# Attention into a gated feed-forward kernel: batch 2's casts moved to steps 34 to 38 and shared by two engines, a check moved to step 17, and a first weight load of four column blocks

## The chip, the cores and the metric

The kernel runs on one core of a Trainium2 chip. The metric is the device time of one execution in microseconds (us). Runs of one kernel are compared by their median. A profiled execution leaves a trace; its span is the time from the first to the last recorded instruction.

The core's engines run their own instruction queues, each in order, and wait for each other through semaphores: TensorE (PE) multiplies, VectorE (DVE), ScalarE (ACT) and GpSimd (POOL) work elementwise, and SyncE (SP) issues transfers. ScalarE and GpSimd issue transfers too, in their own order among their other instructions.

## The reference

Eight batches of eight heads, 576 positions, 64 wide. Each head has causal attention with a decay taken from `s`; the heads' outputs side by side give 4608 rows of 512, which go through an RMS norm and a gated feed-forward layer of width 1536.

```python
scores = scale * np.matmul(q, k.transpose(0, 1, 3, 2))
cum = np.cumsum(np.maximum(s, 0.0), axis=-1)
bias = -(cum[:, :, :, None] - cum[:, :, None, :])
scores = np.where(causal, -1000000000.0, scores + np.minimum(bias, 0.0))
attn = softmax(scores)                       # exp of the scores less their maximum, over the sum
x = (attn @ v).transpose(0, 2, 1, 3).reshape(4608, 512)
...
xn = x / np.sqrt(np.mean(x * x, axis=-1, keepdims=True) + 1e-06) * rms_g
g = xn @ w_gate
out = (g * (1.0 / (1.0 + np.exp(-g))) * (xn @ w_val)) @ w_out
```

All inputs and the output are float32. The kernel multiplies in bfloat16.

## The kernel before, in words

**Chunks and steps.** The 4608 rows form nine chunks of 512, worked through by `ffn(c)` one after another. A chunk has 12 pairs of groups on TensorE, the gate group (L737) and the value group (L746), four products of 512 columns each, and then an output part of four row blocks with 12 products each (L759). A group fills one of four PSUM buffers `psF`. ScalarE makes `T` from the gate group (tanh, L740), VectorE makes `U` from `T` and the same buffer (L749) and `Ht` from `U` and the value group (L742, L754); the output part reads `Ht` block by block, and ScalarE takes its result out (L764). So a buffer of the ring of four comes free when `U` or `Ht` has read it.

Between the groups the attention of later batches is woven in. `ffn` calls `step()` 36 times in a chunk: after each group, and three times in each block of the output part. Steps are numbered through (`slot`); steps 1 to 36 belong to chunk 0, 37 to 72 to chunk 1. In steps 30 to 33 of chunk 0 the GpSimd list is left out.

**What a step does.** It writes, in this order: what the last score step left over; one scaling of a finished row block (`x_scale`, L386, VectorE) with its transpose by DMA on SP (`xt_dma`, L397); one entry of ScalarE's list `act_side`; one transpose of the next batch's queries or keys by DMA on SP (`kq_dma`, L179) where no scaling moved; an entry of the load list `v_side` in odd steps, of GpSimd's list `pool_side`, then TensorE's attention work (`place`), and an entry of VectorE's list `dve_side`. Each list is first in, first out; an entry goes when its condition holds, otherwise the list waits. All of this is fixed when the program is written: a step is a place in the engines' orders, and at run time an engine stands only for data.

**Attention work on TensorE.** `do_s` makes a score step (L275) in the single buffer `psS`, ScalarE takes the exponentials (L299), and GpSimd masks the diagonal block (`affine_select`, L308). `do_av` multiplies with the values (L341, L347), VectorE divides (L354, L356), the sum of squares is taken on ScalarE (L363) or, for the first blocks, on VectorE (L367), and GpSimd makes the row factor (`alpha`, L376 and L379), which `x_scale` needs. Rows go to `xnT` by a DMA transpose, but for block (1, 3) by TensorE (`do_xt`, L406, evicted by L415). `need(c)` sees to it that a chunk's last block is in `xnT` before the chunk starts.

**Batch 2's keys and queries.** They are loaded as float32 into `kq32` by GpSimd's queue (`load2`, L129 and L135; `w` is 1 for q, 0 for k) and cast to bfloat16 into `kqn` (`cast_x`, L153, five for q; `cast`, L145, five for k). `casts(2)` puts all ten on GpSimd's list: those of q from eight steps after their load, those of k behind them. `kqn` is shared by batches 0 and 2, so the casts must come after the check of batch 0. When q is done, `over(1)` frees five `kq_dma` of batch 2, at most one in two steps, and the load of batch 3's q from ScalarE's queue; `over(0)` does the same for the keys, which TensorE transposes (`do_t`, L192, L200) from step 41 on. A load entry that `early` has put up goes only in the first 23 steps of a chunk, and three steps after the load before it.

The steps of this kernel, followed through the conditions, are: casts of q in steps 25 to 29, of k in 34 to 38; `kq_dma` of batch 2 in 33, 35, 37, 42 and 44; score steps of batch 2 from step 46; loads of batch 3 in 37, 40, 43 and 46, its casts from 47 to 57.

**The check.** `check(b)` keeps the largest magnitude of what was cast: one `check_mag` (L418) and two `check_max` (L424) of VectorE, in odd steps. For batch 0's keys they come in steps 9, 11 and 13.

**The weights.** Before chunk 0, GpSimd's queue loads w_gate's column blocks 0 to 3 (exclusive) and later 3 to 6 (`load_w`, L771); the rest follows in step 1. Gate group fb of chunk 0 reads block fb.

Of the kernel before, what the change touches and what calls it, by code (L numbers as in the profile page):

```python
# [12 lines left out]
AF = mybir.ActivationFunctionType  # L13
# [13 lines left out]
def kernel(  # L27
# [12 lines left out]
    nc = tc.nc  # L40
    B, H, S, D = q.shape
# [20 lines left out]
    wg_sb = pers.tile([128, CC, DF], BF16, name="wg_sb")  # L62
# [84 lines left out]
    def cast_x(eng, b, w, hp):  # L147

        if hp < HP:
            o = kqn[:, b % 2, w, 0:4].rearrange("p r h d -> p (r h d)")[:, hp * 512:hp * 512 + 512]  # L150
            o = o.rearrange("p (r h d) -> p h r d", r=4, h=2)
            i = kq32[:, w, 2 * hp:2 * hp + 2, 0:256].rearrange("p h (r d) -> p h r d", d=D)
            eng.tensor_copy(out=o, in_=i)  # L153
        else:
            cast(eng, b, w, 4, 5)

# [24 lines left out]
    def load_v(b, c):  # L181
        n = rows(c)
        nc.gpsimd.dma_start(  # L183
            out=v_sb[0:n, b % 2, c, :, 0:64],
            in_=v[b, :, c * 128:c * 128 + n, :].rearrange("h p d -> p h d"))
# [241 lines left out]


    SLOTS = 36
    slot = [0]  # L430
    first, chunk = [0], [0]
    done = {}
# [10 lines left out]
    pool_side, dve_side, v_side, act_side = [], [], [], []  # L443
# [5 lines left out]
    def ready(lag, *key):  # L449
        return at(*key) + lag <= slot[0]  # L450
# [16 lines left out]
    def check(b, ws=(1, 0)):  # L467
        t = slot[0] + (8 if b >= KB else 0)

        def when(w):  # L470
            if b < 2:
                return slot[0] % 2 and chunk[0] == b and slot[0] > 8
            return phase() >= 25 and slot[0] >= t and (w == 0 or ready(0, "cast", b, 1))
        dve_side.extend((lambda w=w: when(w), f) for w in (ws if b < KB else (0, 1)) for f in (
            lambda w=w: check_mag(b, w), lambda: check_max(0), lambda: check_max(1),
            lambda w=w: done.__setitem__(("check", b, w), slot[0])))
# [18 lines left out]
    def casts(b):  # L495

        def key(c):
            load_k(b, c)  # L500
            done["K", b, c] = slot[0]
            if c == NSC - 1:
                check(b)

        def over(w):
            done["cast", b, w] = slot[0]
            if b + 1 < B and (w == 1 or b + 1 < KB):
                loads(b + 1, w, early, 4)
            if w == 1:
                x_seq.extend((b, ww, c) for c in range(NSC) for ww in ((1, 0) if b >= KB else (1,)))  # L510
            else:
                done["cast", b] = slot[0]
                check(b)

        def free(w):
            return ready(0, "check", b - 2, w) and (
                ready(0, "T", b - 2) if w == 0 and b < KB + 2 else
                b < XB + 2 or ready(4, "X", b - 2, w, 4))
        if b >= KB:
            pool_side.extend((lambda: free(0) and slot[0] % 2 == 0, lambda c=c: key(c)) for c in range(NSC))  # L520
        fns = [(1, lambda r=r: cast_x(nc.gpsimd, b, 1, r)) for r in range(NSC)]
        if b == 2:
            fns[-1] = (1, lambda: (cast_x(nc.gpsimd, b, 1, NSC - 1), over(1)))
        else:
            fns += [(1, lambda: over(1))]
        if b < KB:
            fns += [(0, lambda r=r: cast(nc.gpsimd, b, 0, r, r + 1)) for r in range(NSC)]
            fns += [(0, lambda: over(0))]
        pool_side.extend((lambda w=w: ready(8 if b == 2 else 7, "raw", b, w) and free(w), f) for w, f in fns)

    def after_tail(b):
        if b + 2 < B:
# [129 lines left out]
    def step(bare=False):  # L662
# [15 lines left out]
        run_side(act_side)  # L678

        if not moved and x_seq and slot[0] - last["X"] >= 2 and not (  # L680
                scaled[0] < len(x_list) and ready(1, "AV", *x_list[scaled[0]], 1)):
            b, w, c = x_seq[0]
            if (ready(2, "cast", b, 1) and ready(1, "S", b - 2, 4, 0)
                    and (w == 1 or ready(7, "K", b, c))):
                x_seq.pop(0)
                kq_dma(b, w, c)
                done["X", b, w, c] = last["X"] = slot[0]
                if b >= KB and (w, c) == (0, NSC - 1) and b + 2 < B:
                    casts(b + 2)
# [79 lines left out]
    def load_w(src, dst, f0, f1):  # L769
        fs = slice(f0 * 128, f1 * 128)  # L770
        nc.gpsimd.dma_start(out=dst[:, :, fs],  # L771
                            in_=src[:, fs].rearrange("(cc p) f -> p cc f", p=128))
# [79 lines left out]
    with tc.manual_schedule():  # L852
# [63 lines left out]
        load_v(0, 2)  # L916
        load_v(0, 3)
        load_v(0, 4)
        load_w(moe_w_gate, wg_sb, 0, 3)
        do_t((0, 0, 0), pT=psT(), dve=False)  # L920
        do_t((0, 1, 0), pT=psF16(), dve=False)
        stir(2)
# [57 lines left out]
        norms += [do_av((0, 3, 1), psT32(), act=True, apart=True)]  # L980
        norms[3](False)
        alpha(3, 4)
        load_w(moe_w_gate, wg_sb, 3, 6)
        warm(4)
        for qb in range(4):
            x_scale(0, qb, gq)
# [16 lines left out]
        def load2(w):  # L1003
            load_kq(nc.gpsimd, 2, w)
            load_kq_tail(nc.gpsimd, 2, w)
            done["raw", 2, w] = slot[0]

        def put(queue, n, *fns):
# [12 lines left out]
        put(v_side, 7, lambda: (load_v(1, 0), load_v(1, 1)))  # L1021
        put(v_side, 11, lambda: (load_wout(0), load_wout(6)))
        later(v_side, 0, [
            lambda: load_v(1, 2), lambda: load_v(1, 3), lambda: load2(1), lambda: load_v(1, 4),
            lambda: load2(0)])

        check(0, (0,))
# [194 lines left out]
```

## Time and profile before

| what | value |
|---|---|
| runs | 371.28, 367.72 and 371.75 us; median 371.28 |
| profiled execution | 367.71 us, span 366.1 us |
| TensorE products busy | 346.9 us, 95% of the span |
| VectorE, ScalarE, GpSimd busy | 275.2, 237.6, 179.5 us |
| chunk 0 on TensorE | from 26.47 to 69.98 us |
| TensorE's clock | 0.996 of full speed |

A line of the timeline has the start and the duration in us, the engine, the line of the kernel, the operation with what it writes and reads, how many of the same kind were merged, and in brackets the idle time of the engine before it with what ended it. A line of the waits says who waited for whom, the total in us, how often, and the longest. The busy time of TensorE counts a product up to its modelled end, while the next one has already started, so that gaps show better between starts.

### The profile page before, as it was taken

Reading aid. Unit: us, or ns where it says so; the run is one execution under the profiler, and the core shown is the slowest. Engines: PE = TensorE matmul, PEld = TensorE weight load, DVE = VectorE, ACT = ScalarE, POOL = GpSimd, SP = SyncE. Lnnn points to the kernel's source line nnn. Section 1 sums busy time; section 2 is a strip of 40 time slices with the busy share of each in tenths; the row PEclk is TensorE's granted clock in tenths of the full one; section 3 lists DMA queues with packets and bytes.
Section 4 is the critical chain, followed back from the end, with each engine's and each line's share of the span. In section 5 each row is a group of like instructions: output and inputs, shape, how many; then the busy total and the mean of one; then the engine's idle time right before and its main releaser. Section 6 shows DMA issues by size and latency. Waiting matters only on the chain. (4 is left out here: it accounts for less than half of the span.)

```text
span 366.1 us, 6930 instructions
## 1 busy us (share of the span) xinstructions
PE 346.9 (95%) x2337; PEld 161.4 (44%) x2383; DVE 275.2 (75%) x523; ACT 237.6 (65%) x614; POOL 179.5 (49%) x288
## 2 busy tenths in 40 slices
PE   5989999899999999999999999999999999999992
PEld 2444445443444444444444444444444444444441
DVE  6696997599887889789989789884588557827820
ACT  3978876367885788776787776777677644223311
POOL 7959766949556465879648923732222200000000
PEclk9999999999999999999999999999999999999998
DMA  7999999999969399949969944981300130020011
GB/s 232 134 234 245 172 207 216 176 217 208 195 138 107 67 191 142 166 114 167 164 196 166 152 103 109 114 90 55 105 14 17 43 109 1 0 88 29 1 60 60
DMA packets 124096, 45.81 MB, mean 125 GB/s; under 512 B 103956, under 2 KB 118808, under 8 KB 124056
## 3 DMA queue, kind: packets, MB, share of 16 engines
q0 software_dynamic: 62688, 14.29, 48.4%
q1 hardware_dynamic: 51872, 23.80, 32.2%
q10 hardware_dynamic: 9496, 7.23, 8.3%
q8 instruction: 19, 0.31, 0.4%
q14 instruction: 21, 0.17, 0.2%
HBM read 37.90 MB, written 9.44 MB: 129 GB/s over the span
## 5 line engine op out<-in xcount | busy, mean ns | idle before, releaser
L299 ACT ACTIVATE E<-psS,biasK 128x256 bf16<-128x256 f32 (+3 forms) x328 | 107.3, 415 | 19.7 <-PE psS L275 19.3
L737 PE MATMUL psF<-xnT,wg_sb 128*128 128x512 bf16 x418 | 109.9, 380 | 2.2 <-DMA wg_sb<-in_moe_w_gate_dram 0.5
L746 PE MATMUL psF<-xnT,wv_sb 128*128 128x512 bf16 x419 | 110.1, 379 | 1.2 <-DVE U L749 0.3
L759 PE MATMUL psF<-wout_sb,Ht 128*128 128x512 bf16 x416 | 99.7, 379 | 0.6
L749 DVE SCALAR_TENSOR_TENSOR U<-T,psF 128x512 bf16<-128x512 f32 x108 | 73.6, 682 | 30.6 <-ACT T L740 30.6
L740 ACT ACTIVATE T<-psF 128x512 f32<-128x512 f32 x108 | 64.5, 597 | 43.4 <-PE psF L737 40.9
L308 POOL TENSOR_SCALAR_AFFINE_SELECT E<-E 128x512 bf16<-128x512 bf16 x64 | 45.2, 706 | 83.2 <-ACT E L299 82.8
L742 DVE TENSOR_TENSOR Ht<-U,psF 128x512 bf16<-128x512 bf16 x99 | 67.7, 684 | 7.0 <-PE psF L737 0.5
L737 PEld LDWEIGHTS <-wg_sb 128*128 128x128 bf16 x432 | 38.7, 98 | 46.3 <-issue 6.5
L746 PEld LDWEIGHTS <-wv_sb 128*128 128x128 bf16 x432 | 38.6, 98 | 43.0 <-issue 5.0
L759 PEld LDWEIGHTS <-Ht 128*128 128x128 bf16 x432 | 38.7, 98 | 42.0 <-issue 2.3
L764 ACT ACTIVATE osb<-psF 128x512 f32<-128x512 f32 x36 | 21.4, 595 | 35.6 <-PE psF L759 29.5
L386 DVE SCALAR_TENSOR_TENSOR xs_sb<-x_sb,al_all,g_row 128x512 bf16<-128x512 bf16 (+1 forms) x36 | 29.9, 829 | 13.7 <-POOL al_all L379 12.6
L183 POOL DMA_DIRECT2D v_sb<-in_v_dram x40 | 35.8, 897 | 0.3 <-PE psAV L347 0.2
L363 ACT ACTIVATE xs_sb<-x_sb 128x512 bf16<-128x512 bf16 (+1 forms) x37 | 23.5, 636 | 16.8 <-DVE x_sb L356 16.4
L424 DVE TENSOR_TENSOR acc<-acc,mag 128x1280 bf16<-128x1280 bf16 x32 | 28.4, 899 | 0.2
L275 PE MATMUL psS<-kqT 64*128 64x256 bf16 (+2 forms) x304 | 25.9, 256 | 2.1 <-ACT E L299 0.8
L347 PEld LDWEIGHTS <-E 128*128 128x128 bf16 x320 | 21.7, 98 | 10.1 <-issue 0.2
L379 POOL TENSOR_TENSOR al_all<-al_all,mhalf 128x1 f32<-128x1 f32 (+2 forms) x39 | 22.4, 574 | 3.2
L341 PEld LDWEIGHTS <-E 128*128 128x128 bf16 x256 | 20.0, 98 | 7.7 <-DVE x_sb L356 0.6
L275 PEld LDWEIGHTS <-kqT 64*128 64x128 bf16 x320 | 9.3, 94 | 31.1 <-issue 30.1
L376 POOL TENSOR_SCALAR al_all<-ss_all 128x1 f32<-128x1 f32 (+2 forms) x39 | 10.1, 260 | 24.5 <-ACT xs_sb L363 19.7
(125 smaller groups left out, 301.1 us busy)
## 6 DMA issues: line engine op xcount, KB each, us to landing
out_dram<-osb SPq DMA_DIRECT2D x36, 256.0 KB, 2.3
kq<-in_q_dram ACTq DMA_DIRECT2D x5, 1024.0 KB, 8.4
v_sb<-in_v_dram POOLq DMA_DIRECT2D x32, 128.0 KB, 7.1
kq<-in_k_dram SPq DMA_DIRECT2D x4, 512.0 KB, 5.3
kq<-in_q_dram SPq DMA_DIRECT2D x4, 512.0 KB, 7.2
kqn<-in_k_dram POOLq DMA_DIRECT2D x16, 128.0 KB, 5.0
wout_sb<-in_moe_w_out_dram POOLq DMA_DIRECT2D x2, 768.0 KB, 10.0
kq<-in_q_dram POOLq DMA_DIRECT2D x1, 1024.0 KB, 13.6
```

What stands on the lines that cost most here:

```text
L183: nc.gpsimd.dma_start(out=v_sb[0:n, b % 2, c, :, 0:64], in_=v[b, :, c * 128:c * 128 + n, :].rearrange("h p d -> p h d"))
L275: nc.tensor.matmul(pair[par][:, j * W:j * W + M], lhsT=kT, rhs=qT, start=(j == 0 and not premask), stop=(j == nj - 1))
L299: nc.scalar.activation(out=eo, in_=ei, func=AF.Exp, scale=0.125, bias=biasK[:, kb, bh:bh + 1])
L308: nc.gpsimd.affine_select(out=Ev[:, :, 0:nq], in_=Ev[:, :, 0:nq], pattern=[[0, nh], [1, nq]], compare_op=ALU.is_ge, fill=0.0, base=0, chan ...
L386: nc.vector.scalar_tensor_tensor(out=xs_sb[0:n, (b * NSC + qb) % NX, :], in0=x_sb[0:n, (b * NSC + qb) % NX, :], scalar=al_all[0:n, col:col ...
L424: nc.vector.tensor_tensor(out=acc[:, sl], in0=acc[:, sl], in1=mag[:, sl], op=ALU.max)
L737: nc.tensor.matmul(Gp, lhsT=wg_sb[:, cc, fs], rhs=xnT[:, cc, x0:x0 + DM], start=(cc == 0), stop=(cc == CC - 1))
L740: nc.scalar.activation(out=T, in_=Gp, func=AF.Tanh, scale=0.5)
L742: nc.vector.tensor_tensor(out=Ht[:, fb - 1, :], in0=pend[0], in1=pend[1], op=ALU.mult)
L746: nc.tensor.matmul(Vp, lhsT=wv_sb[:, cc, fs], rhs=xnT[:, cc, x0:x0 + DM], start=(cc == 0), stop=(cc == CC - 1))
L749: nc.vector.scalar_tensor_tensor(out=U, in0=T, scalar=1.0, in1=Gp, op0=ALU.add, op1=ALU.mult)
L759: nc.tensor.matmul(Op, lhsT=Ht[:, fb, tb * 128:(tb + 1) * 128], rhs=wout_sb[:, fb, :], start=(fb == 0), stop=(fb == FB - 1))
```

## The change

The ten casts of batch 2 wait for step 34 (`K2`), one entry per step and engine. ScalarE takes q's head groups 3 and 4 and k's row sets 0, 1 and 2; GpSimd takes q's groups 0, 1 and 2 and k's row sets 3 and 4. The wait for the load's step is gone; the wait for the data stays. `over` is called with the last GpSimd entry of q and of k. The transposes of batch 2 may start one step after that instead of two, and are not held back for the row block (1, 4). The check of batches 0 and 1 starts after step 16 instead of 8 (for batch 1 this changes nothing, its chunk starts later). The first part of w_gate has four column blocks, the second two. On the load list the last value block of batch 1 goes ahead of batch 2's q, which is thereby issued in step 19 instead of 17.

```diff
             i = kq32[:, w, 2 * hp:2 * hp + 2, 0:256].rearrange("p h (r d) -> p h r d", d=D)
-            eng.tensor_copy(out=o, in_=i)
+            if eng is nc.scalar:
+                eng.activation(out=o, in_=i, func=AF.Copy)
+            else:
+                eng.tensor_copy(out=o, in_=i)
...
+    K2 = 34
...
             if b < 2:
-                return slot[0] % 2 and chunk[0] == b and slot[0] > 8
+                return slot[0] % 2 and chunk[0] == b and slot[0] > 16
...
-        pool_side.extend((lambda w=w: ready(8 if b == 2 else 7, "raw", b, w) and free(w), f) for w, f in fns)
+        if b == 2:
+
+            def put2(queue, *fs):
+                queue.extend((lambda: slot[0] >= K2 and free(0) and free(1), f) for f in fs)
+            put2(act_side, *[lambda r=r: cast_x(nc.scalar, b, 1, r) for r in (3, 4)],
+                 *[lambda r=r: cast(nc.scalar, b, 0, r, r + 1) for r in (0, 1, 2)])
+            put2(pool_side, *[lambda r=r: cast_x(nc.gpsimd, b, 1, r) for r in (0, 1)],
+                 lambda: (cast_x(nc.gpsimd, b, 1, 2), over(1)),
+                 lambda: cast(nc.gpsimd, b, 0, 3, 4), lambda: (cast(nc.gpsimd, b, 0, 4, 5), over(0)))
+            return
+        pool_side.extend((lambda w=w: ready(7, "raw", b, w) and free(w), f) for w, f in fns)
...
         if not moved and x_seq and slot[0] - last["X"] >= 2 and not (
-                scaled[0] < len(x_list) and ready(1, "AV", *x_list[scaled[0]], 1)):
+                scaled[0] < len(x_list) and x_list[scaled[0]] != (1, 4) and ready(1, "AV", *x_list[scaled[0]], 1)):
...
-            if (ready(2, "cast", b, 1) and ready(1, "S", b - 2, 4, 0)
+            if (ready(1 if b == 2 else 2, "cast", b, 1) and ready(1, "S", b - 2, 4, 0)
...
-        load_w(moe_w_gate, wg_sb, 0, 3)
+        load_w(moe_w_gate, wg_sb, 0, 4)
...
-        load_w(moe_w_gate, wg_sb, 3, 6)
+        load_w(moe_w_gate, wg_sb, 4, 6)
...
-            lambda: load_v(1, 2), lambda: load_v(1, 3), lambda: load2(1), lambda: load_v(1, 4),
+            lambda: load_v(1, 2), lambda: load_v(1, 3), lambda: load_v(1, 4), lambda: load2(1),
             lambda: load2(0)])
```

## The prediction

> **What bounds the kernel now.** I read four views: the page, TensorE's waits between 26 and 110 us, the timeline of 60 to 70 us, and the landing times of single transfers. Times "at 33.38" are those of the profiled execution before.
>
> ```profile
> span 366.1 us, 6930 instructions
> ...
> PE 346.9 (95%) x2337; PEld 161.4 (44%) x2383; DVE 275.2 (75%) x523; ACT 237.6 (65%) x614; POOL 179.5 (49%) x288
> ```
>
> TensorE sets the time; no other engine is above 75%. So an edit is worth only the TensorE gap that it closes. Where those gaps lie, the waits of 26 to 110 us say (in total, times, longest):
>
> ```profile
> PE psT L406 <- DVE xs_sb L386: 1.0, 1, 1.0
> PE psF L737 <- DMA wg_sb<-in_moe_w_gate_dram: 0.5, 1, 0.5
> PE psF L737 <- DVE U L749: 0.4, 1, 0.4
> PE psF L746 <- DVE U L749: 0.3, 1, 0.3
> PE psF L737 <- DMA xnT<-xs_sb: 0.3, 1, 0.3
> PE psF L737 <- ACT xnT L413: 0.3, 1, 0.3
> PE psT L217 <- DVE xnT L415: 0.2, 1, 0.2
> ```
>
> Six of the seven lie in chunk 0 or at its end, one in chunk 1. From 110 us on TensorE idles about 1 us up to the last chunk, so nothing big is to be had there. These rows understate the gaps, because a product is counted busy until its modelled end, 0.38 us after its start. I measure from start to start instead: four 512-column products take 0.87 (33.38 to 34.25), four transposes 0.22 (34.25 to 34.47), eight value products 0.25, four 0.13, and a score step 0.33 before the next group starts (49.76 to 50.09).
>
> The longest gap has a story, which the timeline of 60 to 70 us tells (start, duration, what; idle before it and what ended it):
>
> ```profile
> 60.55 0.61 POOL L153 CAST kqn<-kq 128x512 bf16<-128x512 f32 x1 [1.16 <-DMA kq<-in_q_dram]
> ...
> 61.57 0.19 ACT L363 ACTIVATION_READ_ACCUMULATOR xs_sb<-x_sb 128x1 f32 x1
> ...
> 61.69 1.72 POOL L153 CAST kqn<-kq 128x512 bf16<-128x512 f32 x3
> 63.50 0.19 POOL L376 TENSOR_SCALAR al_all<-ss_all 128x1 f32<-128x1 f32 x1
> 64.28 0.60 POOL L145 CAST kqn<-kq 128x512 bf16<-128x512 f32 x1
> 64.97 0.51 POOL L376 TENSOR_SCALAR al_all<-ss_all 128x1 f32<-128x1 f32 x1
> 66.15 1.12 DVE L386 SCALAR_TENSOR_TENSOR xs_sb<-x_sb,al_all,g_row 128x512 bf16<-128x512 bf16 x1 [0.72 <-POOL al_all L379]
> 67.33 0.40 PE L406 MATMUL psT<-ident_bf,xs_sb 128*128 128x128 bf16 x4 [1.02 <-DVE xs_sb L386]
> ```
>
> The sum of squares of block (1,2) is ready at 61.76, but GpSimd, in order, is in the casts of batch 2 until 63.4; its factor comes at 63.50. Block (1,3) queues behind that and one more cast. So its scaling starts at 66.15, stretched to 1.12 us beside the factors and casts (0.74 where GpSimd is idle), and TensorE's transposes wait.
>
> **Part 1, w_gate.** Column block 3 now comes with the second part, issued at 24.3 and 9.1 us on its way, so it lands at 33.4. Group 3 could start at 32.42 + 0.22 = 32.64 and starts at 33.38. With block 3 in the first part (issued 14.3, landed after 6.8) the **0.74 us** go. Bounds of the price: the queue behind carries a third more, between 0 and 6.8/3 = 2.3 us. w_val's first half (issued 16.1, 8.9 on its way: 25.0) is needed at 27.33, so even 2.3 is covered. The first keys of batch 1 (21.6 + 5.3 = 26.9) are cast at 28.02; at 2.3 they would hold ScalarE 1.2 and TensorE's transposes of 30.25 at most 0.5. I take 0, since the part lands 5 us before use, and keep 0.5.
>
> **Part 2, the check in step 17.** One mask and two maxima (0.81, 0.80, 1.25 = 2.86 us of VectorE) leave 36.9 to 45.3, where VectorE is busy 13.68 of 14 us and runs two groups behind. Three TensorE gaps come from that: 41.56 + 0.33 = 41.89 against 42.28 (0.39); 45.52 + 0.13 = 45.65 against 45.91 (0.26); 46.87 + 0.33 = 47.20 against 47.50 (0.30). Sum **0.95**. The work lands in steps 17 to 21 (46.9 to 54). Laying VectorE's instructions out anew there, without the old backlog and with three more of 0.81, the last Ht (56.49 to 57.18 now) ends at about 57.9. The output group needs it as its twelfth product, at 58.84, or 58.6 once the gap of 47.50 is gone: 0.7 us of cover, and 0 lost. Between 36 and 46 the sum of VectorE's work falls from 10.3 to about 7.5 of 10.5 us, so no new gap there.
>
> One row of the old place is a warning: a maximum took 1.25 us beside an affine select (43.80) and, at 83.99, 2.27 beside casts, but 0.80 beside weight loads being issued (40.83). The Trainium skill, "SBUF — State Buffer", section "Who interferes with whom", says that a VectorE instruction with two SBUF inputs contends with GpSimd instructions that read SBUF, not with those that only write. The trace agrees (2.27 against 0.80). By that rule both maxima can meet a select in steps 19 and 21; at 1.25 each the last Ht would be 0.9 later and cost TensorE 0.2.
>
> **Part 3, the casts.** Ten on GpSimd (about 0.61 each) become five there and five on ScalarE. One of 512 columns on ScalarE has no row: one of 256 takes 0.41 and twice that, 0.81, bounds it from above; the 512-column eviction of L764 at 0.60 has the same form, and I take 0.6, together 3.0 us. They fall in steps 34 to 38 (66 to 73), where ScalarE idles 3.45 us before L764 at 69.54, 0.92 before 71.06 and 1.29 before 72.94: free. Without that cover T of chunk 1 slips; the psF ring of four bears about 1.7 us.
>
> GpSimd is free from step 25 to 33. The factor of (1,2) can follow at 61.8 to 62.6, its scaling at 63.2 behind the evictions of (1,3), its transpose at 64.0 instead of 65.46. For (1,3): squares 63.97, factor 64.8, scaling 65.6. TensorE comes at 63.55 + 12 x 0.217 = 66.15: the gap of 67.33 - 66.15 = 1.18 goes. The first group of chunk 1 could start at 69.29 + 0.25 = 69.54 and waits until 69.98 for the transpose of (1,2) (0.44). Its transpose took 4.5 us; 64.0 + 4.5 = 68.5 against 69.54 - 1.18 = 68.36 leaves 0.14. Gain **1.48**.
>
> The loads: q of batch 2 is issued in step 19 instead of 17 (about 50.0 for 46.9). It took 13.6, so 63.6 at most, before step 34. k stays at 54.0 + 11.6 = 65.6, before step 36 (68.5 on this scale). Both are waited for by five ScalarE instructions now, with L764 and T queued behind.
>
> What is late next: batch 2's cast of q ends in step 36, not 29. Its five transposes on SP move from steps 33, 35, 37, 42, 44 to 37, 39, 42, 44, 46 (the (1, 4) exemption lets the second go at 39). SP runs ahead, so the first two start when the casts end, near 69; the third stays behind the transpose of (1,4), as now the fourth does (77.60). Scores of batch 2 keep their steps (46, 50, 53), since the keys' casts end in step 38, one earlier. The second transpose has about 7.7 us, the third 10.3 - 0.5. Landings here were 4.8, 6.3 and 10.3: a wait of 0 (6.3) to 2.6 (10.3 for both). I take **0.3**, near the first.
>
> The loads of batch 3 move three steps (q to 40 and 43, k to 46 and 49), its casts from 47-51 and 53-57 to 50-54 and 56-60. So the maximum of step 49 no longer meets them: it took 2.27 and held the group that could start at 85.51 + 0.87 = 86.38 until 86.91, **0.53**, bounds 0 and 0.53. The tail of batch 4's q misses its last step in chunk 1 (phase below 24) and goes from step 59 to 73; its casts wait behind the key loads anyway, 80 for 79. Later transposes shift by one or two steps, five or more ahead of their scores.
>
> **The sum.** 0.74 + 0.95 + 1.48 + 0.53 = 3.70, less 0.3: 3.4 us. The profiled execution took 367.71 (span 366.1 and 1.6 around it): **364.3**. Its runs are 367.72, 371.28 and 371.75, so the profile is the low one and the median 3.6 above. Part of that spread should be these very waits (GpSimd stood 1.16 us for a transfer at 60.55 with everything behind it), which no longer sit on the path. I carry half over: a median of **366.0**, between 364.3 and 367.9.
>
> **Rivals.** (1) Half of the gain is eaten by VectorE in steps 17 to 24: each instruction of the check at 1.25 and a late factor (L376 waits for VectorE's squares, then holds the selects) make the last Ht about 1.7 us late beyond its cover. 366.0 by the profile, some 367.5 as a median. For it: VectorE is nearly full from 51.3 to 59. Against: 0.7 of cover, and VectorE needs only 2.03 of 2.50 us after 57.5.
> (2) Slower: batch 2's transposes. SP starts them later, among the v loads, q and k of batch 3. TensorE, in order, stands at the score step of 79.74 or 87.87. Each us above 7.7 on the way costs one; from 11.4 us the gain is gone, and at 15 the profile is 367.71 + 3.6 = 371.3, the median 373. For it: one took 10.3 in that traffic. Against: the two issued before it took 4.8 and 6.3, and batch 3's q now starts later.
> (3) Nothing to tell: the gaps close, but ScalarE stands for k in steps 36 to 38. TensorE loses from a landing 4.5 us later than now, all of it from 8 us. Then 367.7, median about 371. Against: the longest landing of such a load is 13.8.
>
> **Numbers.** Forecast 0.62, rivals 0.18, 0.12 and 0.08. One per cent, 3.7 us, is about what a measurement of this kernel can tell from no change. Against 371.28 the line is 367.6: the forecast is below it in most cases (0.53 of 0.62), rival 1 in less than half (0.07): faster 0.6. Above 375.0 only rival 2 comes, and only with landings of some 19 us (0.06): slower 0.06, the rest, 0.34, within. Range 363.0 (all gains, a low median) to 370.0 (rival 1 and part of rival 2).
>
> **What would show it.** Right: L737 no longer waits for wg_sb; no wait of L406 near 66; L376 right behind L363; chunk 1 starting near 66.7 instead of 69.98; no maximum above 1.3 us. Wrong: a wait of L275 for kqT by DMA, of L759 for Ht near 57, or ScalarE waiting for kq.

## The result, and the profile after

| | before | after |
|---|---|---|
| median | 367.76 us (366.56 to 371.75) | 366.12 us (364.10 to 369.53) |
| ratio of the times, 95% interval | | 0.9951 [0.9927, 0.9975] |
| profiled execution | 367.71 us (span 366.1) | 364.69 us (span 363.0) |

The change makes the kernel half a per cent faster. The median of before is 367.76 us over all its runs; of the three shown ahead of the prediction, two lay high (371.28 and 371.75). The profiled execution of before stands at its median, that of after 1.4 us under its own. So the two traces differ by 3.0 us and the medians by 1.6, and what the traces show is compared stage by stage below.

The page after, and TensorE's waits between 26 and 110 us (total, times, longest):

```profile
span 363.0 us, 6976 instructions
...
PE 348.8 (96%) x2383; PEld 160.5 (44%) x2383; DVE 273.4 (75%) x523; ACT 239.8 (66%) x619; POOL 178.2 (49%) x283
```

```profile
PE psT L344 <- DVE x_sb L359: 0.4, 1, 0.4
PE psF L751 <- ACT xnT L416: 0.3, 1, 0.3
PE psF L751 <- DVE rZ L357: 0.2, 1, 0.2
PE psS L278 <- ACT E L302: 0.2, 1, 0.2
```

Lines have moved: L737 is now L751, L759 is L773, L406 is L409, L386 is L389, L376 is L379, L356 is L359. Of the seven rows of before, the waits for `xs_sb`, for `wg_sb`, for `U` (two rows) and for `xnT` by DMA or VectorE are gone by name. The wait for `xnT` by ScalarE stays; it ends as chunk 0 begins. New are the first row, TensorE waiting for VectorE's eviction of `x_sb`, and the third, which stands at the start of chunk 1 and is explained below.

The other engines' busy time has hardly changed (VectorE 275.2 to 273.4, ScalarE 237.6 to 239.8, GpSimd 179.5 to 178.2), so the gain should be idle time of TensorE. Its own busy sums can't be compared: the trace before has 2337 product records and that of after 2383. Where the gain lies, the time from each chunk's first gate product to that of the next says, taken from the timelines:

| chunk | 0 | 1 | 2 | 3 | 4 |
|---|---|---|---|---|---|
| before | 43.51 | 39.19 | 38.73 | 38.38 | 37.84 |
| after | 41.62 | 38.65 | 38.89 | 37.73 | 37.43 |
| difference | -1.89 | -0.54 | +0.16 | -0.65 | -0.41 |

In the trace after, chunk 0 starts 0.32 later (26.79 for 26.47), which arises before the weight load is issued; from chunk 5 on the two differ by no more than 0.1. With that start the sum is -3.0, the difference of the profiles.

The end of chunk 0, in the timeline after (PEld is TensorE's weight load for the product behind it):

```profile
57.88 0.76 PEld L773 LDWEIGHTS <-Ht 128*128 128x128 bf16 x5 [0.55 <-DVE Ht L768]
...
58.41 0.69 DVE L370 SCALAR_TENSOR_TENSOR xs_sb<-x_sb 128x512 bf16<-128x512 bf16 x1
...
59.20 0.19 POOL L379 TENSOR_SCALAR al_all<-ss_all 128x1 f32<-128x1 f32 x1 [2.28 <-DVE rZ L357]
...
60.01 0.62 POOL L311 TENSOR_SCALAR_AFFINE_SELECT E<-E 128x512 bf16<-128x512 bf16 x1
60.07 1.11 DVE L389 SCALAR_TENSOR_TENSOR xs_sb<-x_sb,al_all,g_row 128x512 bf16<-128x512 bf16 x1 [0.41 <-POOL al_all L382]
...
61.31 0.42 DVE L359 TENSOR_TENSOR x_sb<-psT,rZ 128x256 bf16<-128x256 f32 x1
...
61.79 0.20 PE L344 MATMUL psT<-v_sb,E 128*128 128x65 bf16 x1 [0.44 <-DVE x_sb L359]
...
63.73 0.50 POOL L379 TENSOR_SCALAR al_all<-ss_all 128x1 f32<-128x1 f32 x1 [0.34 <-ACT xs_sb L366]
...
64.90 0.75 DVE L389 SCALAR_TENSOR_TENSOR xs_sb<-x_sb,al_all,g_row 128x512 bf16<-128x512 bf16 x1 [0.71 <-ACT E L302]
...
65.83 0.39 PE L409 MATMUL psT<-ident_bf,xs_sb 128*128 128x128 bf16 x4
...
68.41 0.55 PEld L751 LDWEIGHTS <-wg_sb 128*128 128x128 bf16 x4 [0.35 <-DMA xnT<-xs_sb]
68.41 1.04 PE L751 MATMUL psF<-xnT,wg_sb 128*128 128x512 bf16 x4 [0.23 <-DVE rZ L357]
```

GpSimd now makes the factor of the last block, (1, 3), right behind ScalarE's sum of squares (63.73), its scaling ends at 65.65, and TensorE transposes it at 65.83 with no wait. The casts of batch 2 follow behind, from 66.12 on GpSimd and from 65.66 on ScalarE, 0.62 us each. But the chain ahead has a new gap at 61.79: VectorE's squares of block (1, 1) come late (58.41), GpSimd stands 2.28 us for their sum at 59.20 (the bracket names another VectorE row, L357), the scaling that follows takes 1.11 beside an affine select, and the eviction at 61.31 holds the products. The first row shows a smaller wait ahead of it, of the output part for the last `Ht`.

The first group of chunk 1 still starts late, at 68.41, though the bracket of its row names only 0.23 us and VectorE. The row of its weight load, just above, names another releaser: the DMA transposes into `xnT`. The landings agree. Here is the DMA transpose of row block (1, 0) (instructions, their duration in ns, when issued; then the time from issue to landing). Before:

```profile
L397 SPq DMA_TRANSPOSE xnT<-xs_sb x1: 1313/1313/1313, 55.8 to 55.8; - x1
...
DMA to landing us min/median/max: 10.7/10.7/10.7
```

After:

```profile
L400 SPq DMA_TRANSPOSE xnT<-xs_sb x1: 1312/1312/1312, 56.5 to 56.5; - x1
...
DMA to landing us min/median/max: 8.5/8.5/8.5
```

The same view gives the first, large transfer of batch 2's keys by GpSimd's queue (L129), and the block (1, 2). Before, the keys were issued at 54.0 and landed at 54.0 + 11.6 = 65.6, (1, 0) at 66.5 and (1, 2) at 70.0, when chunk 1 began. After, the keys landed at 53.6 + 10.7 = 64.3, (1, 0) at 65.0 and (1, 2), issued at 64.21 and 4.2 us on its way, at 68.4: again the moment at which chunk 1 began. The last products of chunk 0 would have let it begin 0.38 us earlier.

### The profile page after: what moved, and what is told of

Same layout as the page of the kernel before. It is cut to its first block, busy times and chain, and to the rows that moved or that the text cites. A ratio compares the mean times of both kernels' runs of the same rounds, so it can differ in the third digit from the quotient of the medians.

```text
span 363.0 us, 6976 instructions
## 1 busy us (share of the span) xinstructions
PE 348.8 (96%) x2383; PEld 160.5 (44%) x2383; DVE 273.4 (75%) x523; ACT 239.8 (66%) x619; POOL 178.2 (49%) x283
## 5 line engine op out<-in xcount | busy, mean ns | idle before, releaser
L751 PE MATMUL psF<-xnT,wg_sb 128*128 128x512 bf16 x432 | 111.1, 379 | 0.6 <-ACT xnT L416 0.3
L773 PE MATMUL psF<-wout_sb,Ht 128*128 128x512 bf16 x432 | 102.5, 379 | 0.1
L311 POOL TENSOR_SCALAR_AFFINE_SELECT E<-E 128x512 bf16<-128x512 bf16 x64 | 46.5, 727 | 77.5 <-ACT E L302 77.0
L751 PEld LDWEIGHTS <-wg_sb 128*128 128x128 bf16 x432 | 38.7, 98 | 44.9 <-issue 5.6
L773 PEld LDWEIGHTS <-Ht 128*128 128x128 bf16 x432 | 38.6, 97 | 42.4 <-issue 2.3
L389 DVE SCALAR_TENSOR_TENSOR xs_sb<-x_sb,al_all,g_row 128x512 bf16<-128x512 bf16 (+1 forms) x36 | 29.9, 831 | 12.8 <-POOL al_all L382 12.1
L427 DVE TENSOR_TENSOR acc<-acc,mag 128x1280 bf16<-128x1280 bf16 x32 | 26.6, 845 | 0.2
L379 POOL TENSOR_SCALAR al_all<-ss_all 128x1 f32<-128x1 f32 (+2 forms) x39 | 10.7, 274 | 29.7 <-ACT xs_sb L366 22.9
## 6 DMA issues: line engine op xcount, KB each, us to landing
kq<-in_q_dram POOLq DMA_DIRECT2D x1, 1024.0 KB, 10.8
```

Source lines behind the costliest of these rows:

```text
L311: nc.gpsimd.affine_select(out=Ev[:, :, 0:nq], in_=Ev[:, :, 0:nq], pattern=[[0, nh], [1, nq]], compare_op=ALU.is_ge, fill=0.0, base=0, chan ...
L389: nc.vector.scalar_tensor_tensor(out=xs_sb[0:n, (b * NSC + qb) % NX, :], in0=x_sb[0:n, (b * NSC + qb) % NX, :], scalar=al_all[0:n, col:col ...
L427: nc.vector.tensor_tensor(out=acc[:, sl], in0=acc[:, sl], in1=mag[:, sl], op=ALU.max)
L751: nc.tensor.matmul(Gp, lhsT=wg_sb[:, cc, fs], rhs=xnT[:, cc, x0:x0 + DM], start=(cc == 0), stop=(cc == CC - 1))
L773: nc.tensor.matmul(Op, lhsT=Ht[:, fb, tb * 128:(tb + 1) * 128], rhs=wout_sb[:, fb, :], start=(fb == 0), stop=(fb == FB - 1))
```

## The experiments

Each kernel is measured beside runs of the kernel before on the same chip; the ratio is to those. "Stage" is the time of the chunks 0 and 1 together in the profiled execution, from the first gate product of chunk 0 to that of chunk 2: 82.70 us before and 80.27 after. All but the first two are variants of the kernel after.

| kernel | median us | ratio [95%] | stage | chunk 1 waits for `xnT` |
|---|---|---|---|---|
| wg_only | 366.31 | 0.9952 [0.9928, 0.9976] | 82.41 | - |
| check_only | 368.29 | 1.0011 [0.9984, 1.0038] | 82.05 | - |
| casts_only | 365.46 | 0.9925 [0.9901, 0.9949] | 81.42 | 0.77 |
| no_check | 365.29 | 0.9942 [0.9917, 0.9967] | 80.80 | 1.69 |
| half_k | 363.78 | 0.9897 [0.9847, 0.9947] | 79.25 | - |
| check_9 | 365.20 | 0.9915 [0.9878, 0.9951] | 81.56 | 1.34 |
| k_early | 366.26 | 0.9951 [0.9919, 0.9983] | 81.23 | 1.16 |
| k_early_sq | 365.94 | 0.9943 [0.9911, 0.9975] | 80.94 | - |
| pool_only | 374.37 | 1.0172 [1.0131, 1.0213] | 88.90 | 1.75 |
| k_late | 376.57 | 1.0249 [1.0200, 1.0297] | 89.07 | 3.36 |
| k_late_c9 | 372.25 | 1.0150 [1.0094, 1.0206] | 85.60 | 2.29 |
| k_late_c25 | 372.77 | 1.0128 [1.0087, 1.0170] | 88.23 | 2.12 |

### The three parts alone

`wg_only` is the kernel before with the weight load alone:

```diff
-        load_w(moe_w_gate, wg_sb, 0, 3)
+        load_w(moe_w_gate, wg_sb, 0, 4)
...
-        load_w(moe_w_gate, wg_sb, 3, 6)
+        load_w(moe_w_gate, wg_sb, 4, 6)
```

> Before with only the weight part changed (column blocks 0 to 4, then 4 to 6). Measure: from the first gate product of chunk 0 to that of chunk 2, 82.70 us before and 80.27 after; inside it, from chunk 0's first product to gate group 3, 6.91 before and 6.23 after. If the step is worth what the two profiles show, group 3 comes at 6.2 and the stage is 82.0. Rival: the gain is given back at the end of chunk 0, where TensorE waits for GpSimd's factor anyway; then 6.2, but 82.6.

Group 3 starts 6.23 us into chunk 0 instead of 6.91, as in the kernel after. Then TensorE stands 0.5 us at 39.01 for GpSimd's cast of batch 1's data, which itself waited 1.65 us for a load. That load took 14.7 us to land here, 9.3 to 10.0 in the three kernels with the old weight parts, and from 7.6 to 15.7 in those with the new ones: behind a larger weight load it can come late, but the spread is too wide to say by how much.

The three gaps of steps 12 to 17 don't open here, though the check is in its old place. VectorE has caught up by then, in TensorE's wait at 39.01 as it seems, and its second maximum took 0.81 us instead of 1.25. So at the last gate group of chunk 0 the kernel is 1.06 us ahead of before (25.96 us into the chunk for 27.02). At the chunk's end this is lost. GpSimd stands for the load of batch 2's queries, with the casts, the factor and the scaling of (1, 3) behind it:

```profile
60.23 0.61 POOL L153 CAST kqn<-kq 128x512 bf16<-128x512 f32 x1 [2.16 <-DMA kq<-in_q_dram]
```

TensorE comes to the transpose of (1, 3) earlier and waits for the same scaling:

```profile
67.01 0.40 PE L406 MATMUL psT<-ident_bf,xs_sb 128*128 128x128 bf16 x4 [1.36 <-DVE xs_sb L386]
```

These idle times were 1.16 and 1.02 before. The stage is 0.29 us shorter, not 0.7: the rest is handed to the next waits, as the rival had it, at about two thirds of its price. That the median fell by 1.4 us, the trace doesn't explain (its profiled execution took 367.20).

`check_only` is the kernel before with the check alone:

```diff
-                return slot[0] % 2 and chunk[0] == b and slot[0] > 8
+                return slot[0] % 2 and chunk[0] == b and slot[0] > 16
```

> Before with only the check of batch 0's keys moved to step 17. If VectorE's lateness (0.23 before an output product, 0.60 before the value products of block (1,3)) comes from the check alone, the three gaps of steps 12 to 17 (0.88) close and at least the 0.23 appears: stage 82.0 to 82.4 of 82.70, since the factor of block (1,3) is late anyway. Rival, that the lateness in the changed kernel comes from the moved casts or loads: no new gap, stage 81.8.

The three gaps in steps 12 to 17 are gone, so without the check there VectorE isn't late. The check alone doesn't make them, since `wg_only` has it in that place and has none of the three. The wait of TensorE for `xs_sb` grows to 1.26, and a wait of 0.41 for `x_sb` (L341, at 62.20) is new: the same new gap as in the kernel after, here without the moved casts. The stage is 0.65 shorter, within what was expected; 0.45 of it lie ahead of the check, since chunk 0 starts later against the landing of w_gate. It is lost again in chunk 2 of this trace, where the transpose issued at 144.24 took 5.0 us to land (3.2 for its counterpart before). An issue of SP ahead of it had taken 2.73 us (1.46 before); whether that is the cause isn't shown:

```profile
149.26 1.02 PE L737 MATMUL psF<-xnT,wg_sb 128*128 128x512 bf16 x3 [1.43 <-DMA xnT<-xs_sb]
```

`casts_only` is the kernel after with the check back in step 9 and the weights in their old parts.

```diff
-                return slot[0] % 2 and chunk[0] == b and slot[0] > 16
+                return slot[0] % 2 and chunk[0] == b and slot[0] > 8
...
-        load_w(moe_w_gate, wg_sb, 0, 4)
+        load_w(moe_w_gate, wg_sb, 0, 3)
...
-        load_w(moe_w_gate, wg_sb, 4, 6)
+        load_w(moe_w_gate, wg_sb, 3, 6)
```

> The changed kernel with the check back in steps 9 to 13 and the weight parts as before: the casts, the order of loads and the condition of the transposes alone. If VectorE's chain is what cost the 0.60 before the value products of (1,3), that gap and the 0.23 are not there, chunk 1 starts without a wait for the transpose of (1,2), and the stage is 82.70 - 1.18 - 0.44 - 0.53 = 80.6. Rival, that the moved casts or loads cause it: the 0.60 stays and the stage is 81.3 or more.

The third part alone brings as much as the whole change: 0.9925 against 0.9951, with intervals that overlap. So does the weight load alone (0.9952), so the medians don't share the gain out among the parts. The gap for `x_sb` isn't there, as the check isn't in steps 17 to 21; so the moved casts and loads don't cause it. But the stage is 81.42 and not 80.6, because a wait for `xnT` is there:

```profile
69.35 1.04 PE L751 MATMUL psF<-xnT,wg_sb 128*128 128x512 bf16 x4 [0.77 <-DMA xnT<-xs_sb]
```

### What VectorE's new load costs, and what is behind it

`no_check` is the kernel after without the check of batch 0's keys:

```diff
-        check(0, (0,))
+        done["check", 0, 0] = 0
```

> The changed kernel without the three VectorE instructions of the check of batch 0's keys (their maximum is left out of the flag). If the check in steps 17 to 21 makes VectorE late, the gaps of 0.23, 0.60 and about 0.3 go and the stage is 80.27 - 1.1 = 79.2. Rival (GpSimd's order, transfers): 80.1 to 80.3.

Both gaps that I had put down to VectorE go: the transpose of (1, 3) starts 38.11 us into chunk 0 instead of 39.04. Yet in the trace none of it is kept: chunk 0 takes 42.15 us for 41.62, and the stage 80.80 for 80.27 (79.2 was expected); the median is a little lower than that of after. TensorE stands at the start of chunk 1:

```profile
69.28 1.04 PE L751 MATMUL psF<-xnT,wg_sb 128*128 128x512 bf16 x4 [1.69 <-DMA xnT<-xs_sb]
```

It arrives earlier and stands for the DMA transposes. In these traces their landing doesn't follow their issue. From the landings of the keys and of block (1, 2) in these traces (issue, then landing, us):

| kernel | keys landed | (1, 2) issued | landed | after the keys |
|---|---|---|---|---|
| before | 65.6 | 65.46 | 70.0 | 4.4 |
| wg_only | 65.1 | 65.15 | 69.4 | 4.3 |
| check_only | 64.3 | 65.79 | 68.6 | 4.3 |
| casts_only | 65.1 | 63.98 | 69.3 | 4.2 |
| no_check | 65.0 | 62.99 | 69.2 | 4.2 |
| after | 64.3 | 64.21 | 68.4 | 4.1 |

The issue varies by 2.8 us and the distance to the keys by 0.3. (1, 0) likewise lands 0.7 to 0.9 us behind the keys in all six, whether issued at 54.5 or at 56.9. A new theory follows: the transposes of `x`, issued by SP, come through only behind the key load that GpSimd's queue has under way.

One more thing stands in these traces. SP's transfers land in the order of their issue: in `no_check` (1, 0) at 65.7, a store of the output at 66.4, (1, 1) at 68.25, a store at 68.7 and (1, 2) at 69.2. In the eleven kernels that issue the key load ahead of (1, 0), (1, 2) lands 3.2 to 3.6 us behind (1, 0). So the load need only hold (1, 0), and the rest may follow by SP's own order; the runs don't separate the two.

### The new theory: half the key load

`half_k` is `no_check` that loads only four of the eight heads of batch 2's keys:

```diff
-            load_kq(nc.gpsimd, 2, w)
+            load_kq(nc.gpsimd, 2, w, 0, H if w else H // 2)
```

> The kernel without the check of batch 0's keys, and of batch 2's keys only the first four heads are loaded (the others keep old values). In six traces the transpose of block (1,2) landed 4.1 to 4.4 us after batch 2's keys, whenever it was issued (63.0 to 65.8). If the transposes wait for that load, the keys land about 2.5 us earlier, the transposes with them, TensorE's wait of 1.69 at chunk 1's start goes, and the stage from chunk 0's first gate product to chunk 2's is 80.80 - 1.7 = 79.1. Rival (the time of issue and a latency of its own): the wait stays, 80.8.

The transposes are issued 0.6 us sooner, as much as chunk 0 starts sooner in this trace, and spend 3.2 us less on their way. Those of (1, 0) and (1, 2) with the whole load:

```profile
L400 SPq DMA_TRANSPOSE xnT<-xs_sb x1: 1314/1314/1314, 54.9 to 54.9; - x1
...
DMA to landing us min/median/max: 10.8/10.8/10.8
...
L400 SPq DMA_TRANSPOSE xnT<-xs_sb x1: 1191/1191/1191, 63.0 to 63.0; - x1
...
DMA to landing us min/median/max: 6.2/6.2/6.2
```

and with half of it:

```profile
L400 SPq DMA_TRANSPOSE xnT<-xs_sb x1: 1313/1313/1313, 54.3 to 54.3; - x1
...
DMA to landing us min/median/max: 7.6/7.6/7.6
...
L400 SPq DMA_TRANSPOSE xnT<-xs_sb x1: 1407/1407/1407, 62.4 to 62.4; - x1
...
DMA to landing us min/median/max: 3.0/3.0/3.0
```

The keys land at 52.5 + 8.3 = 60.8, the blocks at 61.9 and 65.4. The wait for `xnT` is gone, the stage is 79.25 us, close to the 79.1 of this theory, and 1.55 shorter than with the whole load. So the load's second half costs TensorE these 1.55 us here; the medians differ by as much (363.78 and 365.29). The Trainium skill, "DMA: Bandwidth & Descriptors", section "Issuing engines are not separate DMA queues", says that transfers started by SP, ScalarE or GpSimd run on the same 16 DMA engines and interleave. The traces agree that the queues aren't independent: 10.8 against 7.6 us for one transpose on SP, by the size of a load on GpSimd. They don't show a short transfer coming through in between: (1, 0) lands behind the load in all six kernels of the table above and in `half_k`.

### Moving the key load

If the load is what holds the transposes, it could come behind them, or ahead. `k_late` issues it in step 27 and starts the casts of the keys from step 39:

```diff
-            put2(act_side, *[lambda r=r: cast_x(nc.scalar, b, 1, r) for r in (3, 4)],
-                 *[lambda r=r: cast(nc.scalar, b, 0, r, r + 1) for r in (0, 1, 2)])
+            put2(act_side, *[lambda r=r: cast_x(nc.scalar, b, 1, r) for r in (3, 4)])
+            put2(act_side, *[lambda r=r: cast(nc.scalar, b, 0, r, r + 1) for r in (0, 1, 2)], n=K2 + 5)
...
+        put(pool_side, 27, lambda: load2(0))
...
-            lambda: load_v(1, 2), lambda: load_v(1, 3), lambda: load_v(1, 4), lambda: load2(1),
-            lambda: load2(0)])
+            lambda: load_v(1, 2), lambda: load_v(1, 3), lambda: load_v(1, 4), lambda: load2(1)])
```

(and GpSimd's two casts of the keys likewise). `k_late_c9` and `k_late_c25` are the same with the check of batch 0 from step 9 or 25.

> The changed kernel with batch 2's keys loaded in step 27 instead of 21 and their casts from step 39. If the load holds the transposes, those of (1,0), (1,1) and (1,2) land 4 to 6 us after issue at the latest by 67.5, chunk 1 starts without its wait of 0.38, the stage is 79.9; the scores of batch 2 start one or two steps later at no cost. Rival (VectorE's chain sets the start): 80.3, or more if the keys' casts hold the scores.

> The same with the check of batch 0's keys back in steps 9 to 13. With the transposes out of the way VectorE's gaps count alone: 0.88 come back in steps 12 to 17, 0.23 and 0.60 go: stage 79.9, the same as with the check in step 17. Rival (transposes hold the start anyway): 81.0.

> The same with the check in steps 25 to 29, where VectorE is idle a fifth to a half of the time. The gaps of steps 12 to 17 stay closed and the 0.23 and most of the 0.60 go: stage 79.1 to 79.5 and about 1.0 us less than the changed kernel. Rival (one VectorE instruction of 0.8 there delays the chain squares, factor, scaling as it did from step 17): 80.0 or more.

All three are slower than before, and no stage came near the 79.1 to 79.9 that were expected. Of `k_late`'s transposes, (1, 0), issued at 57.4 before the load, now lands in 4.8 us; but (1, 1), issued at 62.1, takes 9.8, and (1, 2), issued at 65.2, takes 7.3, because the load issued at 61.5 is then under way. TensorE waits longer than ever:

```profile
72.47 1.89 PE L751 MATMUL psF<-xnT,wg_sb 128*128 128x512 bf16 x4 [3.36 <-DMA xnT<-xs_sb]
```

So the remedy failed as the mechanism would have it, had I applied it to the new place too: the hold moves with the load. Behind the wait the clock was lower, too (stretches, their length, busy time and instructions of PE, PEld, DVE, ACT and POOL, granted clock, DMA share, GB/s):

```profile
72.00:74.00 2.00, 1.53 (x4) 0.59 (x5) 0.00 (x0) 0.00 (x0) 0.00 (x0) 0.50 1.58 281
74.00:76.00 2.00, 2.00 (x8) 0.75 (x7) 0.69 (x1) 0.60 (x1) 0.00 (x0) 0.50 1.72 201
```

TensorE ran at half clock until 78 us (the next stretch shows 0.50 too), which is about 3 of the 5.5 us by which chunk 1 is longer (44.18 for 38.65). Waits for casts in the chunk (0.90 and 0.29) and three for exponentials (0.55, 0.43 and 0.37) make 2.5 more; with the clock that is nearly all of it.

`k_early` goes the other way: both loads of batch 2 ahead of batch 1's last value block, so that the keys are issued 4.4 us earlier. `k_early_sq` also moves the squares of block (1, 1) to ScalarE, the late link at 58.41 above.

```diff
-            lambda: load_v(1, 2), lambda: load_v(1, 3), lambda: load_v(1, 4), lambda: load2(1),
-            lambda: load2(0)])
+            lambda: load_v(1, 2), lambda: load_v(1, 3), lambda: load2(1), lambda: load2(0),
+            lambda: load_v(1, 4)])
...
-        act = act or b > 1 or b == 1 and qb > 1
+        act = act or b > 1 or b == 1 and qb > 0
```

(the last two lines in `k_early_sq` alone).

> The changed kernel with the last value block of batch 1 loaded behind batch 2's queries and keys: they are issued in steps 17 and 19. If the key load holds the transposes and the transfer engines are full, the keys land 0.5 to 1.5 us earlier, the transposes with them, and the wait of 0.38 at chunk 1's start goes: 365.7. If the landings don't depend on it: 366.1. Rival: the value block's later landing or the queries' earlier load costs something: over 366.5.

> The same with the squares of block (1,1) on ScalarE instead of VectorE. This takes 0.77 us and one hand-over out of VectorE's chain in steps 24 to 30: the gap of 0.60 before the value products of (1,3) and the 0.23 shrink to under 0.2 in sum, TensorE comes to chunk 1 0.6 earlier, and with the keys' earlier landing the time is 365.2. If the landing binds, 365.7 as without it. Rival: ScalarE, in order, is late with exponentials: 366 or more.

In `k_early` the keys are issued at 49.2 and take 15.1 us, so they land at 64.3, no sooner than in the kernel after. (1, 0) lands at 65.6 and (1, 2) at 69.2, 4.9 behind them: the narrow form of the theory, "keys plus 4.2", doesn't hold. The last load ahead of (1, 0) is now the value block, which landed at 66.0, and (1, 0) came with it. So what holds the transposes is the load traffic ahead of them as a whole; with q in front and the value block behind, its end hardly moves. In `k_early_sq` the gap for `x_sb` is gone, which confirms the chain through VectorE's squares, and this time chunk 1 begins without a wait, 41.13 us behind chunk 0. Chunk 1 gives it back: TensorE waits 0.72 us for exponentials at 105.02 and 0.18 for `kqT`, and the stage is 80.94.

### What the share with ScalarE and the place of the check are worth

`pool_only` puts all ten casts on GpSimd's list, still from step 34:

```diff
-            put2(act_side, *[lambda r=r: cast_x(nc.scalar, b, 1, r) for r in (3, 4)],
-                 *[lambda r=r: cast(nc.scalar, b, 0, r, r + 1) for r in (0, 1, 2)])
-            put2(pool_side, *[lambda r=r: cast_x(nc.gpsimd, b, 1, r) for r in (0, 1)],
-                 lambda: (cast_x(nc.gpsimd, b, 1, 2), over(1)),
-                 lambda: cast(nc.gpsimd, b, 0, 3, 4), lambda: (cast(nc.gpsimd, b, 0, 4, 5), over(0)))
+            put2(pool_side, *[lambda r=r: cast_x(nc.gpsimd, b, 1, r) for r in (0, 1, 2, 3)],
+                 lambda: (cast_x(nc.gpsimd, b, 1, 4), over(1)),
+                 *[lambda r=r: cast(nc.gpsimd, b, 0, r, r + 1) for r in (0, 1, 2, 3)],
+                 lambda: (cast(nc.gpsimd, b, 0, 4, 5), over(0)))
```

> The changed kernel with all ten casts of batch 2 on GpSimd from step 34 (q done in 38, k in 43). GpSimd is free of them between the row factors either way, so chunk 1 starts as in the changed kernel. Batch 2's scores start four steps later (50 for 46). If the share of ScalarE only serves that, and there is slack behind, the time is 366.1 +- 0.5; rival: the later scores meet those of batch 3 or GpSimd's casts meet the row factor of (1,4), and it is 367 or more.

The rival was right: 1.7% slower than before. Its waits between 26 and 118 us:

```profile
PE psF L750 <- DMA xnT<-xs_sb: 2.2, 2, 1.8
PE psS L278 <- ACT E L302: 2.1, 4, 0.7
PE psS L278 <- DMA kqT<-kqn: 1.3, 1, 1.3
```

At one cast per step they take twice as many steps, so batch 2's `kqT` and its exponentials come late for TensorE's fixed order, and chunk 1 takes 45.73 us. The named waits in it make some 4.7 of the 7.1 us; the rest is open. In this place, then, the sharing is worth 8.2 us of medians (374.37 for 366.12).

`check_9` is the kernel after with the check back in step 9.

```diff
-                return slot[0] % 2 and chunk[0] == b and slot[0] > 16
+                return slot[0] % 2 and chunk[0] == b and slot[0] > 8
```

> The changed kernel with the check of batch 0's keys back in steps 9 to 13. If the transposes that wait for batch 2's key load set the start of chunk 1 (landing of the keys + 4.1 to 4.4), the place of the check is worth nothing: start of chunk 1 at the keys' landing + 4.2, the three gaps of 0.88 back, the 0.23 and 0.60 gone, time 366.1 +- 0.5, as the changed kernel. Rival (step 17 is worth its 0.88 of closed gaps): 367.0.

Two of the old gaps return (0.40 at 41.66 and 0.24 at 46.88), the new one for `x_sb` goes, and chunk 1 waits 1.34 us for `xnT`. It starts at 69.23, 4.2 behind the keys' landing at 65.0, as was expected. In the profile chunk 0 is 1.29 us longer than after, but the median is the lowest of all versions that compute the whole result, and below the expected 366.1 +- 0.5: 365.20, 0.9915 [0.9878, 0.9951] against 0.9951 [0.9927, 0.9975]. The intervals overlap, so I don't call it better; but the move of the check isn't shown to earn anything. The trace of after may have been a lucky one: its keys landed at 64.3, those of `check_9`, `casts_only` and `no_check` at 65.0 to 65.1, and its profiled execution lies 1.4 us below its median. That is argued from the traces; more profiles of one kernel would be needed to show it.

## Why the prediction was right, and where it was not

The predicted time was 366.0 us and the measured median is 366.12. That is partly luck: the sum gave a profile of 364.3 (364.69 measured), but its terms add up differently, and the step from profile to median rested on a median of 371.28 that more runs put at 367.76. The gain that I forecast as 5.3 us of medians was 1.6, half a per cent, and not the more than one per cent to which I gave 0.6. Of the signs that I named, chunk 1 starting near 66.7 didn't come (68.41), and a sign of being wrong did: the output part waited for `Ht`, its weight load at 57.88.

- **The weight load.** 0.74 predicted, 0.68 measured in chunk 0 (6.23 for 6.91). The first part landed 7.4 us after issue (6.8 before) and w_val's first half at 26.2, before the 27.65 at which it was needed. Right, and the queue behind cost nothing in this trace; in `wg_only` it cost the 0.5 that I had kept as a bound, at a later load of batch 1 than the one I had worked out.
- **The check, the old place.** 0.95 predicted, 0.88 measured. That the gaps come from the check was too simple: `wg_only` has it in the old place without them.
- **The check, the new place.** This step failed: "0.7 us of cover, and 0 lost". The last `Ht` ends at 57.83, as worked out (about 57.9), but held the first output block by some 0.2 (eight products from 57.02 to 58.97 took 1.95, where before four took 0.87). The cover was worked out against a need at 58.6, which leaves out most of what parts 1 and 2 bring TensorE forward: it came to its twelfth product at about 57.02 + 3 x 0.217 = 57.67. And the squares of (1, 1) ran late, from there the factor, the scaling and the eviction of the next block, 0.60 before the products of 61.79. So 0.8 of the 0.88 were lost again: the mechanism of the first rival, which named the late factor, at about half of its price. `no_check` and `k_early_sq` remove the gap at the two ends of that chain.
- **The maxima.** The warning on stretched maxima didn't apply: both took 0.82 us in steps 19 and 21, and so did the one of step 49 that had taken 2.27 beside casts. Its 0.53 was gained in chunk 1 as predicted (chunk 1: -0.54).
- **The casts and the scaling of (1, 3).** Predicted: factor at 64.8, scaling done at 65.6, transpose at 66.15 without a wait. Measured: factor done at 64.86, then 65.65 and 65.83. The 1.18 us went. A cast on ScalarE took 0.62 (0.6 taken) and held nobody up.
- **The start of chunk 1.** Of 0.44 I left 0.14, from "its transpose took 4.5 us; 64.0 + 4.5 = 68.5". The row was read as a fixed duration. It landed at 68.4, but TensorE came earlier than worked out against it, and 0.38 remained. The landing belongs to the load traffic ahead, not to the issue: `no_check` (issued at 62.99, landed at 69.2) shows it, and `half_k` why. This is also why the parts don't add: whatever brings TensorE to chunk 1 sooner meets the transposes, 0.77, 1.34 or 1.69 us early.
- **Batch 2's transposes, the slower rival.** 0.3 was charged and none was paid: the trace after has no wait for `kqT`. It was near: the third transpose took 9.1 us and landed at 85.2, and the next score step came at 85.76. `pool_only` shows that the rival was real: with q's casts done two steps later and k's five it cost 1.3 us.
- **ScalarE held by the load of the keys, the third rival.** Not seen; the keys had landed at 64.3, ahead of every cast.
- **Behind chunk 1.** "From 110 us on TensorE idles about 1 us, so nothing big is to be had there." It was had, nearly whole. Two waits of before at 151.35 and 204.33 have no counterpart after:

```profile
151.35 0.40 PE L275 MATMUL psS<-kqT 64*128 64x256 bf16 x4 [0.45 <-ACT E L299]
...
204.33 1.02 PE L746 MATMUL psF<-xnT,wv_sb 128*128 128x512 bf16 x4 [0.25 <-DVE Ht L742]
```

The chunks 3 and 4 together take 76.22 us before and 76.20 in `wg_only`, but 75.16 after, in `casts_only`, `check_9` and `no_check`. So these 1.06 us seem to come with the third part. For chunk 4 (0.41) no run speaks against it. For chunk 3 (0.65) `check_only`, which lacks the third part, took 37.82 us for 38.38, just behind its wait of 1.43; so a delay ahead can close that gap too, and its cause isn't shown. At 204.33 the way is seen: before, VectorE's scaling at 202.93 waited 1.46 us for GpSimd's factor with `Ht` queued behind it; in `casts_only` the same scaling waited 0.55. Before, GpSimd started the factor 1.81 us after ScalarE's sum of squares, behind a select and the issues of two loads; in `casts_only` 0.92 after it, behind one issue. So the issues of the later batches' loads have moved by some steps, and the factor comes ahead of them. I had looked at the later steps for losses only.

Summed by chunks, in chunk 0 I was 1.3 us too hopeful (0.8 on VectorE, 0.24 at chunk 1's start, 0.13 in the two sizes), in the later chunks 1.2 too cautious. The later start of chunk 0 (0.32) is in neither.

## What to carry to other kernels

Where a transfer's time from issue to landing changes from run to run, look at what other queues have under way before you take the row as a duration: here the landing followed the loads under way on another engine's queue, and an earlier issue behind them was worth nothing. Savings ahead of such a point don't add; sum them only up to the next thing that lands by its own schedule. And a stretch of an in-order engine from which work leaves has to be weighed against the stretch to which it goes, link by link: 0.88 us saved in one place cost 0.8 in the other. Work out such a cover with every gain that the same sum books ahead of it.

## What the runs showed of the hardware

- A DMA transpose issued on SP at 54.9 us landed at 65.7, 10.8 us later, behind a load of 1 MB that GpSimd's queue had issued 1.8 us before it; with half the load it took 7.6. Issued ahead of the load (`k_late`) one took 4.8. At the end of chunk 0 the transfers of SP landed in the order of their issue in every trace.
- The same key load took 7.5 to 15.1 us to land, by where it stood in the traffic (`k_late_c9` and `k_early`).
- A wait of TensorE was followed by a lower clock in two of three cases. After 3.36 us (`k_late`) the granted clock was 0.50 from 72 to 78 us. After 2.12 (`k_late_c25`) it fell to 0.66 and 0.50 between 72 and 76, after 2.29 (`k_late_c9`) it stayed at 1.00. The Trainium skill, "TensorE: Matmul & The Clock Gate", section "What's actually happening", has the gate watch activity in windows of about 3.4 us that run freely. A lower clock after 2.12 and not after 2.29 would fit that, if the moment counts too. But the 2.12 is shorter than such a window, and why the clock fell after it isn't shown.
- A maximum on VectorE took 2.27 us beside casts before and 0.82 after, when none ran beside it. A scaling took 1.11 us that started 0.06 after GpSimd's affine select (60.07), but 0.76 at 55.68, in the midst of two selects, which took 1.70 together where one alone took 0.64 (50.75). That fits the rule that the prediction cites from the Trainium skill, but it was not always VectorE that took longer.
